# One block's lead for w_out's pieces, their split folded into the norm's scale, and the first transposes two steps later

## The chip, the cores and the metric

The kernel runs on one core of one Trainium2 chip. The metric is the device time of one execution in microseconds. TensorE multiplies matrices and transposes by a matmul with the identity, VectorE and ScalarE do the work on elements, GpSimd (POOL) takes a few small steps, and SyncE (SP) issues nearly all transfers from HBM. Each of these engines works through its own queue in the order in which the program was built.

## The reference

Attention of 2 x 12 heads over 448 tokens gives x of 896 x 768. Two feed-forward blocks follow; the change lies in the first:

```python
h = x @ w_in                                   # 896 x 1024
e = np.exp(h - h.max(-1, keepdims=True))
solu = h * e / (e.sum(-1, keepdims=True) + 1e-09)
ln = (solu - mean) / np.sqrt(var + 1e-06) * g_ln
x2 = ln @ w_out                                # 896 x 768
```

The second block is `(silu(x2 @ w_gate) * (x2 @ w_val)) @ w_out2`. The weights come as 64-bit floats.

## The kernel before

Every matmul operand is kept as two 32-bit words, a high one (rounded to the format that TensorE reads) and a low one (what the rounding left), and a product is made of three matmuls: high by high, high by low, low by high (`mm3`).

**Tiles.** The 896 tokens are seven blocks of 128, t = 0 to 6. `ff1_h(t)` makes h_t, two PSUM banks of 128 x 512, in six steps of six matmuls, one step for each 128 columns of x; the last step also issues the tail: maxima (VectorE), the negated maximum, two exponentials with their sums (ScalarE), the sum and its reciprocal, the product e_t = exp * 1/sum * h (VectorE, two halves), mean and variance, a power on GpSimd, and the norm of e_t in place. For t below 5 the variance comes from VectorE's statistics, for 5 and 6 from two squares on ScalarE; the norm itself is VectorE's for t below 4 and ScalarE's from 4 on.

`ff1_T(t)` transposes the normed e_t (eight 128 x 128 transposes into the two banks lt_t_0 and lt_t_1) and writes high (ScalarE) and low words (VectorE) into `lA` (blocks 0 to 2), `lB` (3 and 4) or `lC`, which is part of `y` (5 and 6).

`ff1_x2(j)` makes 128 columns of x2, j = 0 to 5, for the 384, 256 and 256 tokens of lA, lB and lC: 24 matmuls each, over eight pieces of w_out. `load_w_out(j)` prepares these: two transfers of 512 rows (i = 0, 1) into one of two `raw` buffers; `f32` turns the 64-bit words into 32-bit ones (ScalarE takes the magnitude; VectorE clamps, shifts and twice joins words) in one of two `f32` buffers; then, before the change, ScalarE scales each of the four 128 x 128 pieces in place by the norm's factors `gt`, ScalarE copies the 128 x 512 to the high words, VectorE subtracts to get the low ones. The tiles of w_out have three buffers, so w_out 3 lies where w_out 0 lay.

**Order.** Up to the end of attention the program keeps the order in which it is written. From line 541 on, `in_order` is off and the build's scheduler sorts each engine's instructions; the list `steps` (lines 563 and 568 to 574) sets their rank, so that a moved entry moves instructions on all engines. `pin=True` keeps the first steps of `f32` where they are written. The buffers `h`, `lt` and the x2 accumulators share eight PSUM banks.

In the second list the entries `wo[2]` to `wo[5]` stand one block ahead of their use:

```python
steps = x2[0][0] + x2[0][1] + wo[2] + x2[1][0] + T5 + x2[1][1] + T6 + x2[0][2] + x2[1][2]
for j in range(2, KD):
    if j + 1 < KD:
        steps += wo[j + 1]
```

In the names of rows a number counts tiles: `e_5_1760` is e of block 5, `wo_1_0` the second w_out's first half, `sm_t` the small sums of block t. In the profile's rows these numbers are left out.

Of the kernel before, what the change touches and what calls it, by code (L numbers as in the profile page):

```python
# [5 lines left out]
F32 = mybir.dt.float32  # L6
# [3 lines left out]
AF = mybir.ActivationFunctionType  # L10
ALU = mybir.AluOpType
# [25 lines left out]
class Kernel:  # L37
# [379 lines left out]
    def load_w_out(self, j):  # L417

        w = self.wos[j] = self.wo.tile([128, 2, self.K1, 128], F32R, name=f"wo_{j}", tag="wo")
        for i in range(2):  # L420
            c = slice(4 * i, 4 * i + 4)
            src = self.w_out[i * 512:(i + 1) * 512, j * 128:(j + 1) * 128].rearrange("(f p) d -> p f d", p=128)
            f = self.f32(self.load64(src, f"wo_{j}_{i}"), f"wo_{j}_{i}", pin=True).rearrange("p (f d) -> p f d", f=4)
            for m in range(4):
                self.A.activation(f[:, m], f[:, m], AF.Copy, scale=self.gt[:, 4 * i + m:4 * i + m + 1])
            self.hi_act(w[:, 0, c], f)
            self.lo_dve(w[:, 1, c], f, w[:, 0, c])

    def ff1_x2(self, j, get, N, o):

# [75 lines left out]
    def run(self):  # L506
        nc = self.nc
        KD, K1, K2, F1 = self.KD, self.K1, self.K2, self.F1
# [19 lines left out]
        w = [self.w_in_steps(i) for i in range(2 * KD)]  # L528
# [5 lines left out]
        h = [self.ff1_h(t) for t in range(7)]  # L534
# [16 lines left out]
        T = [self.ff1_T(t, lambda: lA, 128 * t) for t in range(3)]  # L551
# [5 lines left out]
        T3, T4 = self.ff1_T(3, lambda: lB, 0), self.ff1_T(4, lambda: lB, 128)  # L557
        T5, T6 = self.ff1_T(5, lambda: lC, 0), self.ff1_T(6, lambda: lC, 128)
        wo = [[(0.0, lambda j=j: self.load_w_out(j))] for j in range(KD)]
        blocks = ((lambda: lA, 384, 0), (lambda: lB, 256, 384), (lambda: lC, 256, 640))  # L560
        x2 = [[[self.ff1_x2(j, *blocks[n])] for n in range(3)] for j in range(KD)]

        steps = h[1] + T[0] + h[2] + T[1] + h[3][:2] + T[2] + h[3][2:] + h[4][:3] + wo[0] + h[4][3:] + wo[1] + h[5][:5] + T3 + h[5][5:] + h[6][:2] + T4 + h[6][2:]
        for _, f in steps:
            f()
        X = [self.slot(f"wi{u}", [128, 6144], f"x2_{u}") for u in range(2)]
        self.x2 = [X[j // 3][:, j % 3 * 1792:(j % 3 + 1) * 1792].rearrange("p (u n) -> p u n", u=2) for j in range(KD)]
        steps = x2[0][0] + x2[0][1] + wo[2] + x2[1][0] + T5 + x2[1][1] + T6 + x2[0][2] + x2[1][2]
        for j in range(2, KD):
            if j + 1 < KD:  # L570
                steps += wo[j + 1]
            if j >= KD - 2:
                steps += [(0.0, lambda i=j - KD + 2: self.load_gv(0, i))]
            steps += x2[j][0] + x2[j][1] + x2[j][2]
# [76 lines left out]
```

## Time and profile before

| | |
|---|---|
| median of 3 runs | 508.88 us (508.77 to 511.54) |
| the profiled execution: time | 509.66 us |
| its span, first to last instruction | 507.9 us |
| mean granted TensorE clock | 0.992 |
| TensorE busy | 98% of the span |
| VectorE busy | 69% |
| ScalarE busy | 51% |

Attention fills the span to about 121 us, h and x2 lie from there to about 242 us, the second feed-forward block behind. In the profile a wait is the idle time of an engine before an instruction, put down to the instruction that ended it. The chain that ended last names, for each moment, what the end of the kernel hung on. Nearly all matmuls are issued by one helper, so all of them have line 29; rows are told apart by tile names: `x` on `lA`, `lB` or `y` is a matmul of x2, `h` one of h, `lt` a transpose.

### The profile page before, as it was taken

To read this page: it belongs to the slowest core of one execution; us is meant where nothing else is said; L and a number is where in the kernel's file an instruction comes from. 1 tells how busy PE (TensorE), PEld (TensorE's weight loads), DVE (VectorE), ACT (ScalarE), POOL (GpSimd) and SP (SyncE) were. 2 spreads that over 40 slices of the span, in tenths; PEclk is the share of its full clock that TensorE was granted. 3 is DMA by queue.
4 is the path that set the end of the run, shared out by engine and by line. 5 is a ranking of instruction groups with operands and counts; after the bars stand their busy time and mean duration, and the time that the engine had idled before them with its cause. 6 is when DMAs were issued, how large, how long until landed. Compare 5 with 4: busy or idle time off the path is not lost.

```text
span 507.9 us, 7456 instructions
## 1 busy us (share of the span) xinstructions
PE 496.3 (98%) x2920; PEld 411.3 (81%) x2920; DVE 348.0 (69%) x625; ACT 256.7 (51%) x388; POOL 20.7 (4%) x63
## 2 busy tenths in 40 slices
PE   6999999999999999999999999999999999999996
PEld 5454444446788899999999988889999889999996
DVE  2788888873778895677899999897997868200000
ACT  2999999990313696474545454353444434100000
POOL 1111111110000000000000000000000000000000
PEclk8999999999999999999999999999999999999999
DMA  8955555320000222145354545435243525111111
GB/s 169 218 127 151 132 151 129 91 70 2 0 1 0 82 85 84 43 146 165 125 176 136 185 127 162 149 124 161 98 148 94 168 80 157 31 32 31 32 31 32
DMA packets 66916, 52.40 MB, mean 103 GB/s; under 512 B 35904, under 2 KB 62272, under 8 KB 66880
## 3 DMA queue, kind: packets, MB, share of 16 engines
q1 hardware_dynamic: 65184, 50.90, 35.5%
q10 hardware_dynamic: 1664, 1.02, 0.6%
q8 instruction: 23, 0.38, 0.3%
q14 instruction: 13, 0.11, 0.1%
q0 software_dynamic: 32, 0.00, 0.0%
HBM read 49.16 MB, written 2.75 MB: 102 GB/s over the span
## 4 chain that ended last, share of the span: by engine, by line
PE 93%; DMA 2%; ACT 2%; DVE 2%; issue 0%; ACTq 0%; POOL 0%; POOLq 0%
PE o L29 17%; PE g L29 17%; PE v L29 17%; PE x L29 10%; PE h L29 10%; PE pv L29 8%; PE sc L29 7%; PE S L29 4%; PE T L29 2%; DMA q<-in_q_dram 1%; PE lt L29 1%; DVE sm L29 1%; ACT P L29 1%; ACT wo L29 1%; DMA wo_raw<-in_moe_w_out_dram 1%; DVE e L29 0%
## 5 line engine op out<-in xcount | busy, mean ns | idle before, releaser
L29 PE MATMUL g<-x,y 128*128 128x512 f32 (+1 forms) x432 | 91.3, 363 | 0.0
L29 PE MATMUL v<-x,y 128*128 128x512 f32 (+1 forms) x432 | 90.5, 362 | 0.0
L29 PEld LDWEIGHTS g<-x,y 128*128 128x128 f32 x432 | 78.3, 188 | 8.8
L29 PEld LDWEIGHTS v<-x,y 128*128 128x128 f32 x432 | 78.2, 188 | 8.5
L29 PE MATMUL h<-wi,x 128*128 128x512 f32 x252 | 58.8, 392 | 0.0
L29 PEld LDWEIGHTS h<-wi,x 128*128 128x128 f32 x252 | 46.8, 188 | 10.9 <-issue 1.4
L29 PE MATMUL o<-x,a 128*128 128x384 f32 x294 | 52.4, 336 | 0.0
L29 PEld LDWEIGHTS o<-x,a 128*128 128x128 f32 x294 | 51.2, 188 | 0.0
L29 ACT ACTIVATE P<-sc,c 112x896 f32<-112x896 f32 x48 | 45.6, 999 | 3.1 <-PE sc L29 2.7
L29 ACT ACTIVATE P<-P,cp 112x1792 f32<-112x1792 f32 x24 | 43.1, 1795 | 0.5
L29 PE MATMUL pv<-P,v 112*64 112x448 f32 x192 | 41.2, 551 | 0.0
L29 PEld LDWEIGHTS sc<-ks 64*112 64x112 f32 x288 | 24.1, 176 | 19.6 <-issue 8.5
L493 ACT ACTIVATE ob<-o 128x384 f32<-128x384 f32 x14 | 6.9, 491 | 65.0 <-PE o L29 65.0
L29 PE MATMUL sc<-ks 64*112 64x448 f32 x288 | 36.8, 387 | 1.0 <-ACT P L29 1.0
L29 PE MATMUL o<-y,a 128*128 128x384 f32 x189 | 34.3, 337 | 0.0
L29 PEld LDWEIGHTS o<-y,a 128*128 128x128 f32 x189 | 33.2, 188 | 0.1
L29 PEld LDWEIGHTS pv<-P,v 112*64 112x64 f32 x192 | 11.7, 136 | 23.9 <-issue 16.6
L29 PE MATMUL x<-lA,wo 128*128 128x384 f32 x144 | 28.1, 337 | 0.9 <-ACT wo L29 0.9
L29 PEld LDWEIGHTS x<-lA,wo 128*128 128x128 f32 x144 | 24.3, 188 | 1.1 <-ACT wo L29 1.1
L29 ACT ACTIVATE a<-sg 128x384 fp32r<-128x384 f32 (+1 forms) x24 | 13.9, 578 | 21.9 <-DVE sg L469 21.8
L29 DVE SCALAR_TENSOR_TENSOR w<-w_raw,w 128x768 uint32<-128x768 uint32 (+1 forms) x26 | 23.1, 892 | 0.4
L29 ACT ACTIVATE wv<-wv_raw 128x768 f32<-128x768 f32 x12 | 10.9, 910 | 24.6 <-DMA wv_raw<-in_moe_w_val_dram 24.6
(97 smaller groups left out, 682.5 us busy)
## 6 DMA issues: line engine op xcount, KB each, us to landing
wg_raw<-in_moe_w_gate_dram SPq DMA_DIRECT2D x12, 768.0 KB, 4.3
wv_raw<-in_moe_w_val_dram SPq DMA_DIRECT2D x12, 768.0 KB, 4.3
w_raw<-in_moe_w_out_dram SPq DMA_DIRECT2D x11, 768.0 KB, 4.5
wi_raw<-in_moe_w_in_dram SPq DMA_DIRECT2D x12, 512.0 KB, 4.2
wo_raw<-in_moe_w_out_dram SPq DMA_DIRECT2D x12, 512.0 KB, 3.5
v<-in_v_dram SPq DMA_DIRECT2D x24, 112.0 KB, 2.8
k<-in_k_dram SPq DMA_DIRECT2D x23, 112.0 KB, 4.1
q<-in_q_dram SPq DMA_DIRECT2D x23, 112.0 KB, 4.6
```

The lines of the kernel that those rows point to most:

```text
L29: i = f(*a, **k)
L493: nc.scalar.activation(ob, acc, AF.Copy)
```

## The change

It has three parts. `load_w_out` no longer scales in place: ScalarE scales each 128 x 128 piece straight into the high words, and VectorE makes the low words of each piece in one instruction, (f * g) - high, so that the copy of 128 x 512 and the subtraction of 128 x 512 go and four instructions on 128 x 128 come. In the first list T[0] stands behind the first two steps of h[2] instead of behind h[1]. In the second list w_out 3 to 5 stand one block earlier: w_out 3 before the last block of x2_1, and w_out j + 2 before x2_j.

```diff
             for m in range(4):
-                self.A.activation(f[:, m], f[:, m], AF.Copy, scale=self.gt[:, 4 * i + m:4 * i + m + 1])
-            self.hi_act(w[:, 0, c], f)
-            self.lo_dve(w[:, 1, c], f, w[:, 0, c])
+                g, hi = self.gt[:, 4 * i + m:4 * i + m + 1], w[:, 0, 4 * i + m]
+                self.A.activation(hi, f[:, m], AF.Copy, scale=g)
+                self.V.scalar_tensor_tensor(w[:, 1, 4 * i + m], f[:, m], g, hi.bitcast(F32), op0=ALU.mult, op1=ALU.subtract)
...
-        steps = h[1] + T[0] + h[2] + T[1] + h[3][:2] + T[2] + h[3][2:] + h[4][:3] + wo[0] + h[4][3:] + wo[1] + h[5][:5] + T3 + h[5][5:] + h[6][:2] + T4 + h[6][2:]
+        steps = h[1] + h[2][:2] + T[0] + h[2][2:] + T[1] + h[3][:2] + T[2] + h[3][2:] + h[4][:3] + wo[0] + h[4][3:] + wo[1] + h[5][:5] + T3 + h[5][5:] + h[6][:2] + T4 + h[6][2:]
...
-        steps = x2[0][0] + x2[0][1] + wo[2] + x2[1][0] + T5 + x2[1][1] + T6 + x2[0][2] + x2[1][2]
+        steps = x2[0][0] + x2[0][1] + wo[2] + x2[1][0] + T5 + x2[1][1] + T6 + x2[0][2] + wo[3] + x2[1][2]
         for j in range(2, KD):
-            if j + 1 < KD:
-                steps += wo[j + 1]
+            if j + 2 < KD:
+                steps += wo[j + 2]
```

What this does to the engines' queues is seen at three places. The first is VectorE's queue around the norm of block 1 (`TENSOR_SCALAR e_1`, 128x1024); `lA<-lt_0` are the low halves of block 0's transposes, `TENSOR_REDUCE sm_2<-h_2` the maxima of block 2, and a minus marks the order before, a plus that of the change.

```order
+L29 TENSOR_TENSOR lA_1374<-lt_0_0_1453,lA_1374 128x4x128
+L29 TENSOR_TENSOR lA_1374<-lt_0_1_1460,lA_1374 128x4x128
 L29 BN_STATS sm_1_1421<-e_1_1422 128x6 x2
 L29 BN_AGGR sm_1_1421<-sm_1_1421 128x2
 L29 TENSOR_SCALAR sm_1_1421<-sm_1_1421 128x1 x2
+L29 TENSOR_REDUCE sm_2_1491<-h_2_0_1439 128x1
 L29 TENSOR_SCALAR e_1_1422<-e_1_1422,sm_1_1421 128x1024
-L29 TENSOR_REDUCE sm_2_1491<-h_2_0_1453 128x1
-L29 TENSOR_REDUCE sm_2_1491<-h_2_1_1454 128x1
+L29 TENSOR_REDUCE sm_2_1491<-h_2_1_1440 128x1
```

The two low halves now stand between block 1's product and its statistics (before, they stood ahead of the product), and the maximum of h_2's first half has moved ahead of e_1's norm.

The second place is ScalarE's queue around block 5's exponentials (`e_5<-h_5`), ahead of the transposes of block 4; `wo_1_0<-wo_1_0_raw` is the magnitude of w_out 1's first half. Before:

```order
L29 ACTIVATE lB_1381<-lt_3_1_1746 128x4x128
L29 ACTIVATE e_4_1661<-e_4_1661,sm_4_1660 128x1024
L29 ACTIVATE wo_1_0_1681<-wo_1_0_raw_1679 128x512
L29 ACTIVATE e_5_1760,sm_5_1759<-h_5_0_1707,sm_5_1759 128x512
L29 ACTIVATE e_5_1760,sm_5_1759<-h_5_1_1708,sm_5_1759 128x512
L29 ACTIVATE wo_0_1_1630<-wo_0_1_1630,gt_115 128x128 x4
L29 ACTIVATE wo_0_1613<-wo_0_1_1630 128x512
```

And now, the same place:

```order
L29 ACTIVATE lB_1381<-lt_3_1_1754 128x4x128
L29 ACTIVATE wo_0_1613<-wo_0_1_1632,gt_115 128x128 x4
L29 ACTIVATE e_5_1768,sm_5_1767<-h_5_0_1715,sm_5_1767 128x512
L29 ACTIVATE e_4_1665<-e_4_1665,sm_4_1664 128x1024
L29 ACTIVATE wo_1_0_1685<-wo_1_0_raw_1683 128x512
L29 ACTIVATE e_5_1768,sm_5_1767<-h_5_1_1716,sm_5_1767 128x512
```

The four scalings of w_out 0's second half moved from behind the two exponentials to ahead of them, and the norm of e_4 and a magnitude stand between the two.

The third place is VectorE's queue from block 5's small sums to its product (`e_5,sm_5<-e_5,sm_5,h_5`). Before:

```order
L29 TENSOR_SCALAR sm_5_1759<-sm_5_1759 128x1
L29 SCALAR_TENSOR_TENSOR wo_0_1_1630<-wo_0_1_raw_1628,wo_0_1_1630 128x512
L29 TENSOR_SCALAR wo_1_0_1681<-wo_1_0_1681 128x512 x2
L29 SCALAR_TENSOR_TENSOR wo_1_0_1681<-wo_1_0_raw_1679,wo_1_0_1681 128x512
L29 TENSOR_SCALAR sm_5_1759<-sm_5_1759 128x1
L29 SCALAR_TENSOR_TENSOR wo_1_0_1681<-wo_1_0_raw_1679,wo_1_0_1681 128x512
L29 RECIPROCAL sm_5_1759<-sm_5_1759 128x1
L29 SCALAR_TENSOR_TENSOR e_5_1760,sm_5_1759<-e_5_1760,sm_5_1759,h_5_0_1707 128x512
L29 SCALAR_TENSOR_TENSOR e_5_1760,sm_5_1759<-e_5_1760,sm_5_1759,h_5_1_1708 128x512
```

And now, from the clamp of w_out 1's first half (the first row) on:

```order
L29 TENSOR_SCALAR wo_1_0_1685<-wo_1_0_1685 128x512
L29 TENSOR_REDUCE sm_6_1837<-h_6_0_1785 128x1
L29 TENSOR_SCALAR wo_1_0_1685<-wo_1_0_1685 128x512
L29 TENSOR_SCALAR sm_5_1767<-sm_5_1767 128x1
L29 TENSOR_REDUCE sm_6_1837<-h_6_1_1786 128x1
L29 SCALAR_TENSOR_TENSOR wo_1_0_1685<-wo_1_0_raw_1683,wo_1_0_1685 128x512
L29 RECIPROCAL sm_5_1767<-sm_5_1767 128x1
L29 TENSOR_TENSOR lB_1381<-lt_4_0_1799,lB_1381 128x4x128
L29 TENSOR_TENSOR lB_1381<-lt_4_1_1806,lB_1381 128x4x128
L29 TENSOR_SCALAR sm_6_1837<-sm_6_1837 128x1
L29 SCALAR_TENSOR_TENSOR wo_1_0_1685<-wo_1_0_raw_1683,wo_1_0_1685 128x512
L29 SCALAR_TENSOR_TENSOR e_5_1768,sm_5_1767<-e_5_1768,sm_5_1767,h_5_0_1715 128x512
```

The product of e_5 stood ahead of the maxima of block 6; now both maxima, the words of w_out 1's first half and the low halves of lt_4 (`lB<-lt_4`) stand ahead of it.

In TensorE's queue lt_0 comes behind twelve matmuls of h_2, lt_1 right behind h_2 as before, and the same 60 matmuls of x2 stand between lt_4 and lt_5, in another order among themselves. SyncE's transfers of w_out stand as before.

## Rows read from the trace of the kernel before

**Rows 1.** Page section 1: engine, busy us (share of the span), instructions.

```profile
PE 496.3 (98%) x2920; PEld 411.3 (81%) x2920; DVE 348.0 (69%) x625; ACT 256.7 (51%) x388; POOL 20.7 (4%) x63
```

**Rows 2.** TensorE's waits in the whole span: total us, times, longest.

```profile
PE T L29 <- DMA q<-in_q_dram: 3.7, 1, 3.7
PE sc L29 <- ACT P L29: 1.0, 1, 1.0
PE warm L29 <- DVE z L29: 1.0, 1, 1.0
PE x L29 <- ACT wo L29: 0.9, 1, 0.9
PE lt L29 <- DVE e L29: 0.5, 1, 0.5
PE x L29 <- ACT y L29: 0.4, 1, 0.4
```

**Rows 3.** Timeline 134 to 143 us: start, us, engine, operation, [idle before].

```profile
134.50 1.28 DVE L29 TENSOR_REDUCE sm<-h 128x1 f32<-128x512 f32 x2
...
134.64 1.09 PE L29 MATMUL lt<-ident,e 128*128 128x128 f32 x8 [0.53 <-DVE e L29]
...
136.57 0.21 DVE L29 TENSOR_SCALAR sm<-sm 128x1 f32<-128x1 f32 x1
...
140.06 1.28 DVE L29 BATCH_NORM_STATS2 sm<-e 128x6 f32<-128x512 f32 x2
...
142.69 0.81 DVE L29 TENSOR_SCALAR e<-e,sm 128x1024 f32<-128x1024 f32 x1
```

**Rows 4.** Chain that ended last, in order of time: start, us, what.

```profile
135.73 8.20 PE h L29 x36
...
179.26 0.87 PE lt L29 x8
...
189.24 0.87 PE lt L29 x8
...
190.12 3.78 PE x L29 x26
```

**Rows 5.** Timeline 175 to 186 us, ScalarE and VectorE, same columns.

```profile
175.29 0.67 ACT L29 ACTIVATE e<-h,sm 128x512 f32<-128x512 f32 x1
...
176.62 1.28 ACT L29 ACTIVATE wo<-wo,gt 128x128 f32<-128x128 f32 x4
...
177.87 0.75 DVE L29 SCALAR_TENSOR_TENSOR e<-e,sm,h 128x512 f32<-128x512 f32 x1
...
184.89 1.26 ACT L29 ACTIVATE e<-e,sm 128x1024 f32<-128x1024 f32 x1
```

**Rows 6.** Operations by shape, ScalarE, 130 to 245 us: busy us, mean ns, idle before.

```profile
L29 ACT ACTIVATE wo<-wo_raw 128x512 f32<-128x512 f32 x12 | 7.9, 658 | 0.7 <-DMA wo_raw<-in_moe_w_out_dram 0.7
```

**Rows 7.** The same of VectorE, 130 to 245 us.

```profile
L29 DVE SCALAR_TENSOR_TENSOR wo<-wo_raw,wo 128x512 uint32<-128x512 uint32 x24 | 16.4, 687 | 0.3
...
L29 DVE TENSOR_TENSOR wo<-wo,wo 128x512 fp32r<-128x512 f32 x12 | 8.2, 687 | 6.7 <-ACT wo L29 6.7
...
L29 DVE TENSOR_REDUCE sm<-h 128x1 f32<-128x512 f32 x12 | 7.8, 684 | 0.9 <-PE h L29 0.9
...
L29 DVE TENSOR_SCALAR sm<-sm 128x1 f32<-128x1 f32 x28 | 5.4, 200 | 5.6 <-POOL sm L29 2.8 <-ACT e L29 2.6
...
L29 DVE TENSOR_SCALAR wo<-wo 128x512 f32<-128x512 f32 x12 | 5.1, 424 | 2.1 <-ACT wo L29 1.7
...
L29 DVE TENSOR_TENSOR x<-x,x 128x256 fp32r<-128x256 f32 x12 | 5.1, 422 | 4.2 <-ACT x L29 4.0
```

**Rows 8.** Page section 6, transfers: count, KB each, us to landing.

```profile
wo_raw<-in_moe_w_out_dram SPq DMA_DIRECT2D x12, 512.0 KB, 3.5
```

**Rows 9.** Stretches of us: busy us per engine, granted TensorE clock, DMA.

```profile
13.00:14.00 1.00, 1.00 (x7) 0.48 (x4) 0.95 (x2) 0.89 (x2) 0.00 (x0) 0.50 0.96 191
17.00:18.00 1.00, 0.58 (x6) 0.45 (x6) 0.97 (x3) 1.00 (x2) 0.00 (x0) 1.00 1.00 281
```

## Prediction

> **What bounds the kernel.** I read the page's busy shares first: TensorE works in 98% of the span [rows 1], so little can be saved beside it. Then TensorE's own waits: six, 7.5 us together [rows 2]. The 3.7 us for q, the 1.0 for the first scores and the 1.0 for the warm-up zeros lie ahead of all that changes. What the change can touch is 0.5 us before lt_0, 0.9 us where `x2_3` waits for w_out, and 0.4 us where `x2_0`'s last block waits for `y`: 1.8 us. To this comes that eight transposes after a wait take 1.09 us [rows 3] instead of 0.87 [rows 4]. The most to be gained is thus about 2 us, 0.4%. The loss has no such bound: everything from 121 to 242 us is one chain of matmuls, TensorE takes them in the order of the program, and a normed tile that comes late stops it. So I followed the two chains that end in a normed tile and that the change reorders, `e_1`'s and `e_5`'s, through VectorE and ScalarE.
>
> **Part 1: lt_0 behind 12 matmuls of h_2.** TensorE ends h_1 at 134.64 - 0.53 = 134.11 us [rows 2, 3]. Now 12 matmuls of h_2 follow, 2.7 us, and cover the rest of e_0's norm, which lt_0 awaited until 134.64. Gain: 0.53 + (1.09 - 0.87) = 0.75 us. If that cover were gone, this and no more would be lost.
>
> But lt_1 comes right behind h_2 and needs e_1 normed. TensorE is there at 134.11 + 8.20 (36 matmuls of h_2) + 0.87 (lt_0) = 143.18 [rows 4]. Before, e_1's norm began at 142.69 [rows 3]. Three changes in VectorE's order move it:
> - The low halves of lt_0 no longer stand between h_1's maxima (end 134.50 + 1.28 = 135.78) and the step after them (136.57 before): that step starts at 135.82, 0.75 earlier [rows 3].
> - They now stand between e_1's product and its statistics: two of 0.69 [rows 7], 1.28 together if they overlap as the two statistics do [rows 3], and 1.20 net of the joint behind them. That much later.
> - The maximum of h_2's first half now stands ahead of the norm. That half is ready at about 143.0, the norm's factors at 143.1; the maximum takes 0.68 [rows 7], part of it before the factors are there. 0.50 later.
>
> So the norm starts at 142.69 - 0.75 + 1.20 + 0.50 = 143.64, takes 0.81, ends at 144.45, and lt_1 starts at 144.51: a wait of 1.33, plus 0.22 for transposes from rest. Cost 1.55; with the gain of 0.75 TensorE is **0.80 us later** from here on. At lt_2, by the same steps, e_2 is normed at 153.1 and wanted at 144.51 + 1.09 + 8.20 = 153.8: no further wait.
>
> **Part 2: w_out split while it is scaled.** ScalarE loses a 128x512 copy per piece, twelve times. VectorE loses one 128x512 subtraction of 0.69 and gets four on 128 columns that no row shows. Below: 0.20, a step on one column; above: 0.42, 256 columns [rows 7]. From 256 to 512 columns the time grows by 0.265, so 128 take 0.29, and I use that since it lies on the line of the nearest rows. Four, each overlapping the next by 0.08, are 0.9 us: 0.2 more per piece (-0.1 to +0.75 at the bounds). "VectorE: DVE Perf Modes" of the Trainium skill gives, in its section on the TRN2 errata, a fixed 58 cycles per instruction, by which 128 columns are an estimated 0.19 us, and the wait found below would be some 0.4 shorter; it also warns that small tiles pay the fixed part each time.
>
> By itself that moves little. What matters is where the pieces stand in the queues. Times are now those of the changed kernel, 0.80 late.
> - Before, ScalarE did both exponentials of e_5 from 175.29 on and scaled w_out behind them, from 176.62 [rows 5]. Now the four scalings of w_out 0's second piece (1.28) stand ahead, and wait for VectorE's words until about 174.6. Then follow the first exponential, e_4's norm (1.26 like e_5's), the next piece's magnitude (0.66, [rows 6]) and the second exponential: e_5's sums are there at 179.1 instead of 176.7.
> - VectorE stands at the clamp of w_out 1 until that magnitude ends (178.3), and next at the maximum of h_6. Its first half ends 0.2 before h_6, so at 179.26 + 0.80 - 0.2 = 179.87 [rows 4]. From there to the end of e_5's product stand twelve instructions: two maxima (0.68), a shift (0.42), three steps of 0.20 at most, two word operations (0.69), the low halves of lt_4 (0.69), the two products (0.75) [rows 5, 7]. 6.6 us, less 0.08 at each of eleven joints: 5.7. The product ends at 185.6; before, it began at 177.87 [rows 5].
> - Then e_5's mean (186.1). ScalarE is in e_6's exponentials, four scalings, a magnitude and an eviction until 187.2; the two squares (like the exponentials, 0.67 each and a read) end at 188.7. VectorE's next small steps end at 189.3, GpSimd's power at 190.0, a word operation and the factors at 191.0; ScalarE's norm takes 1.26 [rows 5]. e_5 is normed at 192.3, and **lt_5 starts at 192.35**.
>
> TensorE wants lt_5 at 189.24 + 0.80 = 190.04 [rows 4], behind the same 60 matmuls. The wait is 2.3 us, with the slower transposes **2.5 us**. With the bounds of the four small subtractions on this chain, 2.2 to 3.1; if VectorE gains 1 us elsewhere, 1.5.
>
> **Part 3: pieces one block sooner.** Behind lt_5 the engines have caught up: e_6 is normed 3.6 us before lt_6, and the 0.37 us for `y` shrink to 0.2, so -0.2. The third buffer of w_out is that of w_out 0, so piece 3's low halves wait for the end of x2_0's last block (205.6). But x2_3 now starts at 214.8, and its second piece, scaled at about 215.6, is wanted 12 matmuls of 384 and 10 of 256 columns later, some 3.2 us (26 such take 3.78, [rows 4]), at 218.0. The wait of 0.88 goes: -0.9, with 2.4 us to spare. SP issues the transfers in the same order, each when one of two raw buffers is free; the tightest is w_out 2's first, which lands 3.5 us [rows 8] after 184.3, at 187.8, and is wanted at 188.9. The gate and value weights lie under x2_4 and x2_5, some 20 us, as before; without that cover each would cost a transfer's time. Behind 242 us TensorE waits for nothing [rows 2], so that stage only starts later.
>
> **Sum.** -0.75 + 1.55 + 2.5 - 0.2 - 0.9 = +2.2 to +2.3 us: span 507.9 to 510.2. The profiled execution took 509.66 us, the median of the three runs is 508.88; from the median, **511.2 us**.
>
> **The rivals.**
> - *All is gained* (faster): e_5's chain isn't blocked, and -0.75 - 0.37 - 0.88 = -2.0 gives 506.9 us. It decides if e_5's product ends before 183.3 and e_1's norm before 143.2. For it: VectorE idles at 143.7 before, so there is some room. Against it: the order puts VectorE's waits for a magnitude and for h_6 ahead of e_5's sum.
> - *Only the first new wait stays*: lt_5 waits 0 to 0.3, so +0.80 + 0.1 - 0.2 - 0.9 = -0.2, 508.7 us. For it: my walk has some 40 joints, and 0.06 less at each would do. Against it: at two places VectorE stands still, and there no joint is gained.
> - *TensorE's clock falls before lt_5.* At the start TensorE rested 3.7 us [rows 2], and until 14.6 us it then ran at a granted clock of 0.50, the 1.2 GHz level [rows 9]. After the rest of 1.0 before 17.4 it stayed at 1.00 [rows 9]. A rest of 2.3 lies between. From 9.06 to 14.6 half of 5.5 us was lost, so +2.7: 513.9 us. "TensorE: Matmul & The Clock Gate" of the Trainium skill, section "What's actually happening", calls the half rate the default that activity lifts; no row here shows a rest between 1.0 and 3.7.
>
> **How the numbers follow.** The forecast (a loss of 1 to 3.5 us, 509.9 to 512.4) gets 0.60; only the first wait 0.16; all gained 0.08; the clock 0.16. The range from 508.4 to 513.9 leaves out the 506.9 and half of the clock's case, about 0.16. 1%, about what a measurement of this kernel can tell from no change, is 5.1 us. No case reaches 503.8, and half of the clock's lies beyond 513.9: faster 0.01, same 0.91, slower 0.08.
>
> **What would show it.** TensorE's waits should list two for `lt`: about 1.3 near 144.5, and about 2.3 near 192.3 on ScalarE's `e`; none of `x` on `wo`. lt_0 should start at about 136.8 with no wait, and VectorE stand idle near 177 and 179. I am wrong if lt_5 starts before 191, if TensorE still waits for w_out, or if the granted clock falls behind 192.

## The result and the profile after

The changed kernel takes 512.14 us (median of 20 runs, 510.55 to 515.73) and the kernel before 508.91 beside it (20 runs, 508.59 to 512.65). The ratio is 1.0054, with a 95% interval from 1.0039 to 1.0070: a loss of 2.75 us (2.0 to 3.6), which counts as the same time here. A ratio in this text is taken over all runs of both kernels; it is not the quotient of the two medians, which is 1.0063 here (3.2 us). The forecast was 511.2 us, a loss of 2.2 to 2.3.

The profiled execution spans 510.6 us, 2.7 more than before. Page section 1 of the kernel after, which answers to [rows 1] (busy us, share of the span, instructions): TensorE's work is the same, VectorE has 4.8 us more, ScalarE 6.5 us less.

```profile
PE 496.1 (97%) x2920; PEld 411.0 (80%) x2920; DVE 352.8 (69%) x661; ACT 250.2 (49%) x376; POOL 21.9 (4%) x63
```

TensorE's waits of the kernel after, which answer to [rows 2] (total us, times, longest):

```profile
PE T L29 <- DMA q<-in_q_dram: 4.4, 2, 3.8
PE lt L29 <- ACT e L29: 2.3, 1, 2.3
PE lt L29 <- DVE e L29: 1.3, 1, 1.3
...
PE x L29 <- ACT y L29: 0.2, 1, 0.2
```

Against [rows 2], lt_0's 0.5 and `x2_3`'s 0.9 on w_out are gone, and two waits of normed tiles are new: 1.3 and 2.3 us. The two rows left out, for the first scores and the warm-up, and the wait for q lie in the start, which differs from one execution to the next. To leave it out I measure between two places of TensorE's chain: the first 18 matmuls of h_0 and the first of g. These are the rows of the chain and of the timeline, first before, then after (start us, us, what):

```profile
112.54 4.30 PE h L29 x18
242.20 3.29 PE L29 MATMUL g<-x,y 128*128 128x384 f32 x18
```

```profile
113.13 4.30 PE h L29 x18
244.98 3.29 PE L29 MATMUL g<-x,y 128*128 128x384 f32 x18
```

From the one to the other it is 129.66 us before and 131.85 after: **+2.19**. The changed execution reached h_0 0.59 us later already, so 0.59 is to be taken off its times before they are set against the prediction's. Behind g both take the same (507.9 - 242.2 = 265.7, 510.6 - 245.0 = 265.6).

The first new wait, on VectorE and TensorE (timeline: start, us, engine, operation, [idle before]):

```profile
139.90 1.28 DVE L29 TENSOR_TENSOR lA<-lt,lA 128x512 fp32r<-128x512 f32 x2
141.10 1.28 DVE L29 BATCH_NORM_STATS2 sm<-e 128x6 f32<-128x512 f32 x2
...
143.61 0.68 DVE L29 TENSOR_REDUCE sm<-h 128x1 f32<-128x512 f32 x1
144.21 0.81 DVE L29 TENSOR_SCALAR e<-e,sm 128x1024 f32<-128x1024 f32 x1
...
145.07 1.09 PE L29 MATMUL lt<-ident,e 128*128 128x128 f32 x8 [1.32 <-DVE e L29]
```

lt_0's low halves (139.90) stand ahead of e_1's statistics and h_2's maximum (143.61) ahead of its norm, and lt_1 starts behind that norm. The second, on ScalarE, VectorE and TensorE, same columns:

```profile
175.19 1.28 ACT L29 ACTIVATE wo<-wo,gt 128x128 fp32r<-128x128 f32 x4 [3.40 <-DVE wo L29]
176.37 0.67 ACT L29 ACTIVATE e<-h,sm 128x512 f32<-128x512 f32 x1
...
178.72 0.67 ACT L29 ACTIVATE e<-h,sm 128x512 f32<-128x512 f32 x1
```

```profile
175.72 1.13 DVE L29 SCALAR_TENSOR_TENSOR wo<-wo,gt,wo 128x128 fp32r<-128x128 f32 x4
178.85 0.43 DVE L29 TENSOR_SCALAR wo<-wo 128x512 f32<-128x512 f32 x1 [1.99 <-ACT wo L29]
180.45 0.69 DVE L29 TENSOR_REDUCE sm<-h 128x1 f32<-128x512 f32 x1 [1.17 <-PE h L29]
...
184.69 0.74 DVE L29 SCALAR_TENSOR_TENSOR e<-e,sm,h 128x512 f32<-128x512 f32 x1
```

```profile
191.67 1.24 ACT L29 ACTIVATE e<-e,sm 128x1024 f32<-128x1024 f32 x1 [0.20 <-DVE sm L29]
...
192.96 1.09 PE L29 MATMUL lt<-ident,e 128*128 128x128 f32 x8 [2.33 <-ACT e L29]
```

Against [rows 5], the four scalings of w_out 0 have moved ahead of e_5's exponentials; VectorE stands still 1.99 us for a magnitude (178.85) and 1.17 for h_6's maximum (180.45), and begins e_5's product at 184.69 instead of 177.87.

### The profile page after: what moved, and what is told of

Its sections match the earlier page's. It is cut to its first block, busy times and chain, and to the rows that moved or that the text cites. A ratio compares the mean times of both kernels' runs of the same rounds, so it can differ in the third digit from the quotient of the medians.

```text
span 510.6 us, 7490 instructions
## 1 busy us (share of the span) xinstructions
PE 496.1 (97%) x2920; PEld 411.0 (80%) x2920; DVE 352.8 (69%) x661; ACT 250.2 (49%) x376; POOL 21.9 (4%) x63
## 3 DMA queue, kind: packets, MB, share of 16 engines
HBM read 49.16 MB, written 2.75 MB: 102 GB/s over the span
## 4 chain that ended last, share of the span: by engine, by line
PE 90%; DVE 5%; DMA 2%; ACT 1%; issue 0%; POOL 0%; ACTq 0%; SPq 0%; POOLq 0%
PE o L29 17%; PE g L29 17%; PE v L29 17%; PE x L29 10%; PE h L29 8%; PE pv L29 8%; PE sc L29 6%; PE S L29 4%; DMA q<-in_q_dram 2%; PE T L29 2%; DVE sm L29 2%; DVE e L29 1%; PE lt L29 1%; DVE wo L29 1%; ACT e L29 1%
## 5 line engine op out<-in xcount | busy, mean ns | idle before, releaser
L29 ACT ACTIVATE e<-h,sm 128x512 f32<-128x512 f32 x14 | 9.5, 683 | 30.0 <-DVE sm L29 30.0
```

What stands on the lines that cost most here:

```text
L29: i = f(*a, **k)
```

## The experiments

In the table, "h_0 to g" is the distance above less the 129.66 us of before; the columns behind it are TensorE's waits in us (e5 to e7 also wait 0.4 at lt_2). *clock* marks a profile in which the granted clock fell to 0.50 behind such a wait.

| kernel | ratio to before (95%) | h_0 to g | lt_0 | lt_1 | lt_5 | lt_6 | x2_0 on y | x2_3 on w_out |
|---|---|---|---|---|---|---|---|---|
| before | | 0 | 0.53 | 0 | 0 | 0 | 0.37 | 0.88 |
| the change | 1.0054 (1.0039 to 1.0070) | +2.19 | 0 | 1.32 | 2.33 | 0 | 0.25 | 0 |
| e1 part 1 | 1.0003 (0.9985 to 1.0021) | +0.65 | 0 | 1.32 | 0 | 0 | 0.38 | 0.74 |
| e2 part 2 | 1.0068 (1.0047 to 1.0089) | +3.56 | 0.53 | 0 | 2.32 | 0 | 2.32 | 0 |
| e3 part 3 | 0.9966 (0.9948 to 0.9983) | -1.17 | 0.53 | 0 | 0 | 0 | 0.37 | 0 |
| e4 part 2, w_out 1 later | 1.0078 (1.0050 to 1.0105) | +4.23, clock | 0.53 | 0 | 4.10 on w_out ahead of it | 0 | 0 | 0 |
| e5 part 1, order held | 1.0040 (1.0023 to 1.0058) | +3.45, clock | 0 | 0 | 0 | 1.69 | 0.73 | 0.53 |
| e6 = e5 and e3 | 1.0034 (1.0020 to 1.0047) | +2.59, clock | 0 | 0 | 0 | 1.69 | 0.73 | 0 |
| e7 = e6, w_out 2 to 5 split | 1.0020 (1.0007 to 1.0033) | +0.55 | 0 | 0 | 0 | 1.69 | 0.25 | 0 |
| e8 change, w_out 0 and 1 unsplit | 0.9996 (0.9986 to 1.0006) | -0.30 | 0 | 1.31 | 0 | 0 | 0.25 | 0 |
| e9 lt_0 beside lt_1 | 0.9990 (0.9981 to 0.9998) | -0.63 | 0 | 0 | 0 | 0 | 0.37 | 0.91 |
| e10 = e9 and e3 | 0.9955 (0.9942 to 0.9968) | -1.85 | 0 | 0 | 0 | 0 | 0.37 | 0 |
| e11 parts 1 and 2 | 1.0055 (1.0040 to 1.0070) | +3.89, clock | 0 | 1.32 | 2.32 | 0 | 0.25 | 0 |
| e12 the change again | 1.0067 (1.0044 to 1.0090) | +3.72, clock | 0 | 1.31 | 2.32 | 0 | 0.25 | 0 |

**The parts alone.** e1, e2 and e3 each apply one part of the diff to the kernel before: the new `steps` line of the h stage, the new loop in `load_w_out`, and the two lines that give w_out 3 to 5.

> The first edit alone: the first normed tile's transposes behind twelve matmuls of h_2, w_out prepared and issued as before. My theory (order on VectorE): lt_0 waits 0 instead of 0.53 us, lt_1 waits 1.3 us because lt_0's two low halves and h_2's first maximum stand ahead of e_1's norm; with the slower restart of the transposes (0.22 us, gone at lt_0 and new at lt_1) the time is 0.8 us above before (+0.16%, ratio 1.0010 to 1.0025). lt_5 (no wait), x2_3 (0.88 us on w_out) and x_0_640 (0.37 us on y) stay as they are. Rival (the edit does what it says): lt_1 waits 0 and the time is 0.75 us below before (ratio 0.9985). Rival (something beyond the waits makes the whole change dearer than its 2.2 us, its 20 runs lay 3.2 us above before): this part alone already costs over 1.5 us.

The median is 509.55 us against 508.79. The time alone does not decide, since its interval holds no change too; the waits do, and so does the distance of +0.65:

```profile
135.39 1.03 PE L29 MATMUL lt<-ident,e 128*128 128x128 f32 x8
143.20 1.09 PE L29 MATMUL lt<-ident,e 128*128 128x128 f32 x8 [1.32 <-DVE e L29]
```

lt_0 no longer waits, and lt_1 waits 1.32 with w_out prepared as before. So the first new wait belongs to part 1 alone.

> The second edit alone: w_out split into its two halves while the norm's scale is applied, in columns of 128, with the first normed tile and w_out's pieces given where they were. My theory (order): ScalarE takes the four scalings of w_out 0's second piece ahead of e_5's exponentials, VectorE takes the words of w_out 1, both maxima of h_6 and lt_4's low halves ahead of e_5's product, and lt_5 waits 2.3 us on e_5 (2.0 to 2.7), as it did in the whole change; lt_0 keeps its 0.53 us. x2_3's wait of 0.88 us on w_out, which the pieces given sooner removed in the whole change, stays within 0.9 us. Time 2.3 to 2.7 us above before (ratio 1.0045 to 1.0055). Rival (VectorE's added work: 0.45 us in each of twelve pieces is what costs): waits for w_out spread over the x2 stage, at x2_2 and later, 1 us or more in all, and lt_5 waits under 1 us. Rival (no effect): all hidden, within 0.3 us of before.

512.73 us against 508.79. The wait of lt_5 came as expected, but the time lies above what was expected, and two waits were missed: `x2_0`'s last block waits 2.32 us for `y`, and `x2_3` no longer waits for w_out. ScalarE and TensorE in e2:

```profile
200.82 1.28 ACT L29 ACTIVATE wo<-wo,gt 128x128 fp32r<-128x128 f32 x4 [0.96 <-DVE wo L29]
202.00 1.05 ACT L29 ACTIVATE y<-lt 128x512 fp32r<-128x512 f32 x2
...
202.62 0.50 PE L29 MATMUL x<-y,wo 128*128 128x256 f32 x2 [2.32 <-ACT y L29]
```

The same place on ScalarE in the whole change:

```profile
199.48 0.60 ACT L29 ACTIVATE y<-lt 128x512 fp32r<-128x512 f32 x1
200.71 1.28 ACT L29 ACTIVATE wo<-wo,gt 128x128 fp32r<-128x128 f32 x4 [0.63 <-DVE wo L29]
```

In e2 four scalings of w_out 2, which wait for VectorE, stand ahead of both halves of `y`; in the change the first half stands ahead of them. Part 1, which edits only the h stage 60 us earlier, is what sets that order otherwise: e11, parts 1 and 2 without part 3, waits 0.25 there like the change. So the price of part 2 depends on part 1: the parts' distances add to 0.65 + 3.56 - 1.17 = 3.04 and the change has 2.19.

> The third edit alone: w_out 3, 4 and 5 given one block sooner, all else as before. My theory: only x2_3's wait of 0.88 us on w_out goes, every other wait as before (lt_0 0.53, x_0_640 on y 0.2 to 0.4): 0.9 us below before (ratio 0.9975 to 0.9990). Rival (the pieces given sooner get in the way): the steps of w_out 3 stand ahead of e_6's norm or of y's halves on ScalarE and VectorE, lt_6 or x_0_640 waits 0.5 to 2 us more, and the time is the same or up to 1.5 us above before. Rival (the transfer is what is late, not the place): x2_3 still waits 0.5 us or more.

507.49 us against 508.79. The gain is a little more than expected (ratio 0.9966 against 0.9975 to 0.9990). Only that wait is gone, and it is worth 1.17 us, 0.3 more than it lasted. TensorE's rows show most of the 0.3. First before, then e3, the same two matmuls of `x2_3`:

```profile
217.60 0.61 PE L29 MATMUL x<-lA,wo 128*128 128x384 f32 x2 [0.88 <-ACT wo L29]
```

```profile
214.43 1.54 PE L29 MATMUL x<-y,wo 128*128 128x256 f32 x12
215.81 0.51 PE L29 MATMUL x<-lA,wo 128*128 128x384 f32 x2
```

Without a wait the two start 0.16 us before the matmuls ahead of them end (214.43 + 1.54 - 215.81), and they take 0.10 less. A wait loses both: 0.88 + 0.16 + 0.10 = 1.14.

**Order or work.** e4 is e2 with `wo[1]` moved:

```
-        steps = h[1] + T[0] + h[2] + T[1] + h[3][:2] + T[2] + h[3][2:] + h[4][:3] + wo[0] + h[4][3:] + wo[1] + h[5][:5] + T3 + h[5][5:] + h[6][:2] + T4 + h[6][2:]
+        steps = h[1] + T[0] + h[2] + T[1] + h[3][:2] + T[2] + h[3][2:] + h[4][:3] + wo[0] + h[4][3:] + h[5][:5] + T3 + h[5][5:] + wo[1] + h[6][:2] + T4 + h[6][2:]
```

> The second edit alone as in e2 (the split while scaling, all twelve pieces, the same VectorE work), but w_out 1 is given behind h_5 instead of ahead of it. In the new order only four scalings and one subtraction of w_out 0's second piece are left near e_5's exponentials, and of w_out 1 nothing stands ahead of e_5's product or norm; the first maximum of h_6 still does. My theory (what costs in e2 is where w_out 1's steps stand in the two engines' order): lt_5 waits under 0.8 us, 0.5 of it for that maximum, and the time falls by 1.5 us or more against e2, unless w_out 1, now later, is waited for at x2_1 (its first matmuls stand right behind lt_5; if so, a wait of 1 to 4 us shows there on w_out, and the verdict goes by lt_5's own wait). Rival (VectorE's added work of 0.45 us in each piece is what costs): lt_5 still waits 1.5 us or more, the time is as in e2.

513.23 us. e_5's norm, and then TensorE:

```profile
185.15 1.24 ACT L29 ACTIVATE e<-e,sm 128x1024 f32<-128x1024 f32 x1
...
190.25 0.65 PE L29 MATMUL x<-lA,wo 128*128 128x384 f32 x2 [4.10 <-ACT wo L29]
190.71 1.91 PE L29 MATMUL lt<-ident,e 128*128 128x128 f32 x8
```

With all the work of the split, e_5 is normed at 186.39, 8.3 us behind lt_4's start (178.08); in e2 lt_5 starts 12.5 us behind lt_4's (193.41 and 180.93). TensorE came at 190.25 - 4.10 = 186.15, so lt_5 alone would have waited some 0.3 us. So the added work of the split, spread over all pieces, does not by itself make e_5 late; what stands ahead of e_5's steps does. The edit also takes w_out 1's words out of e_5's way, which stood there before as well, so it does not set order against work by itself; the trace of the change does that below. It gains nothing here: w_out 1 is now late itself, `x2_1` stands 4.10 us on it ahead of lt_5, and the clock falls.

e8 undoes the split for w_out 0 and 1 only, in the whole change:

```
+            if j < 2:
+                for m in range(4):
+                    self.A.activation(f[:, m], f[:, m], AF.Copy, scale=self.gt[:, 4 * i + m:4 * i + m + 1])
+                self.hi_act(w[:, 0, c], f)
+                self.lo_dve(w[:, 1, c], f, w[:, 0, c])
+                continue
             for m in range(4):
...
```

> The whole change with one thing undone: w_out 0 and 1 are prepared as before (scaling in place, copy, subtraction of 512 columns), w_out 2 to 5 are split while scaling. The first normed tile and the pieces are as in the change, VectorE's order is free. My theory: e_5's exponentials are ahead of w_out 0's scalings again and its product ahead of h_6's maxima, though the two loads' words still stand ahead of that product; lt_5 waits 0 to 0.6 instead of 2.33, lt_1 keeps its 1.3; time 2.0 to 2.6 us below the change, so -0.3 to +0.5 against before (ratio 0.9990 to 1.0010). Rival (lt_5's wait comes from the first normed tile's new place or the pieces given sooner, not from the split): lt_5 still waits 1.5 us or more and the time is that of the change (ratio 1.005).

508.81 us against 509.10, as expected. One wait of normed tiles is left, lt_1's of 1.31 us.

Eight of the twelve pieces are still split and cost nothing that shows. The whole of lt_5's wait came from the split of w_out 0 and 1, whose steps stand among e_5's. e8 takes back their work and their order together.

**Can part 1's wait be mended?** e5 is e1 with VectorE held in written order over the first 24 steps:

```
-            if self.kernel.in_order:
+            if self.kernel.in_order or (self.kernel.pin_v and self.engine is self.kernel.nc.vector):
...
-        for _, f in steps:
+        for n, (_, f) in enumerate(steps):
+            self.pin_v = n < 24
             f()
+        self.pin_v = False
```

> The first edit alone as in e1, but VectorE keeps the order in which the code is written from h_1 to lt_2's low halves and h_3 (TensorE's and ScalarE's rows stay free): e_1's norm stands ahead of lt_0's two low halves and of h_2's maxima, and e_2's norm ahead of h_3's maxima. The work is the same, and lt_0 stands at the same place behind twelve matmuls. My theory (what costs in e1 is the order on VectorE): lt_0 and lt_1 both wait 0, lt_2 waits 0 to 0.5; time 0.75 us below before (ratio 0.9975 to 0.9995), 1.4 us below e1. Rival (the place itself costs, because the transposes' results take slots or VectorE time that e_1 or e_2 need): lt_1 or lt_2 still waits 1 us or more and the time is not below before.

511.90 us against 509.10: the expectation was wrong. lt_1 does not wait, as I said; but lt_2 waits 0.41, and the loss comes 50 us later. TensorE, then ScalarE, at lt_6:

```profile
196.45 1.09 PE L29 MATMUL lt<-ident,e 128*128 128x128 f32 x8 [1.69 <-ACT e L29]
198.27 0.79 PE L29 MATMUL x<-y,wo 128*128 128x256 f32 x2 [0.73 <-ACT y L29]
```

```profile
193.60 0.49 ACT L29 ACTIVATE x<-x 128x384 fp32r<-128x384 f32 x1 [1.20 <-PE x L29]
193.99 1.27 ACT L29 ACTIVATE wo<-wo,gt 128x128 f32<-128x128 f32 x4
194.15 0.21 DVE L29 TENSOR_SCALAR sm<-sm 128x1 f32<-128x1 f32 x1 [0.44 <-POOL sm L29]
195.16 1.23 ACT L29 ACTIVATE e<-e,sm 128x1024 f32<-128x1024 f32 x1
```

And ScalarE before, with VectorE's step that ends the norm's factors:

```profile
191.19 1.28 ACT L29 ACTIVATE wo<-wo,gt 128x128 f32<-128x128 f32 x4
191.68 0.20 DVE L29 TENSOR_SCALAR sm<-sm 128x1 f32<-128x1 f32 x1
192.38 1.23 ACT L29 ACTIVATE e<-e,sm 128x1024 f32<-128x1024 f32 x1
193.92 0.49 ACT L29 ACTIVATE x<-x 128x384 fp32r<-128x384 f32 x1 [0.30 <-PE x L29]
```

Before, e_6's norm began at 192.38 and ended 1.3 us ahead of lt_6. Four scalings of w_out 2 stand right ahead of it in both kernels. Two things differ: the norm's factors are done at 194.36 instead of 191.88, and a copy of x2's 384 columns, for which ScalarE stands 1.20 us, has moved from behind the norm to ahead of the scalings. TensorE wanted lt_6 at 196.45 - 1.69 = 194.76. With ScalarE free at 194.36 the norm would have ended at some 195.6, so by an estimate 0.9 us of the wait come from the late factors and 0.8 from the scalings behind that copy. Nothing is held at that place: the scheduler chose another order there when only the h stage was changed. And the clock fell behind the two waits.

> A version that could beat both: w_out 3 to 5 given one block sooner as in e3, the first normed tile behind twelve matmuls of h_2 with VectorE held in written order as in e5, and w_out prepared as before (no split while scaling). My theory: the waits of lt_0 (0.53 and 0.22 of slower transposes) and of x2_3 (0.88) both go, x_0_640 keeps 0.2 to 0.4 on y; time 1.6 to 2.0 us below before (ratio 0.9960 to 0.9970), 0.7 below e3. Rival (the freed time turns up as a new wait): lt_6 or x_0_640 waits 0.7 us or more, and the time is that of e3 or above.

510.80 us: the rival named for it came true, with the same two waits as in e5.

> The kernel of e6 with the split while scaling for w_out 2 to 5 only; w_out 0 and 1, whose steps stand among e_5's in the order of ScalarE and VectorE, are prepared as before. So eight of twelve pieces carry VectorE's added 0.45 us and save ScalarE's copy of 0.63. My theory (the split costs by its place among e_5's steps, not by its work): lt_5 waits 0, no wait on w_out in the x2 stage, the time is that of e6 within 0.3 us. Rival (VectorE's added work costs): waits for w_out at x2_2 to x2_5 or a later x_0_640, 0.5 us or more above e6. Rival (ScalarE's saved copies gain): x_0_640's wait on y of 0.37 goes and the time is 0.4 us below e6.

510.26 us. lt_6 waits 1.69 as in e6, which I had not foreseen; `x2_0`'s wait for `y` is 0.25 instead of 0.73 and the clock does not fall. The time is 0.5 us below e6 and not within 0.3, near to what the second rival named (0.4 less, with the wait for `y` gone); how much of it is the clock and how much the saved copies was not taken apart. No wait for w_out shows, so the eight split pieces cost nothing here either.

e9 looks for another place for lt_0, one that leaves the order behind lt_3 alone:

```
-        steps = h[1] + T[0] + h[2] + T[1] + h[3][:2] + T[2] + h[3][2:] + h[4][:3] + wo[0] + h[4][3:] + wo[1] + h[5][:5] + T3 + h[5][5:] + h[6][:2] + T4 + h[6][2:]
+        steps = h[1] + h[2] + T[0] + T[1] + h[3][:2] + T[2] + h[3][2:] + h[4][:3] + wo[0] + h[4][3:] + wo[1] + h[5][:5] + T3 + h[5][5:] + h[6][:2] + T4 + h[6][2:]
```

> The first edit alone, but with lt_0's transposes behind all six steps of h_2, right ahead of lt_1's, instead of behind two (order on VectorE free, w_out as before). In the new order nothing of lt_0 stands ahead of e_1's norm; its two low halves stand behind h_2's maxima, beside lt_1's, where e_2's exponentials are waited for; from lt_3 on both engines' rows stay as before but for a few of w_out 0's. My theory (in e1 lt_0's low halves and h_2's maximum in e_1's chain were the cause; in e5 it was the new order behind lt_3): lt_0 and lt_1 wait 0, e_2's exponentials come 1.1 to 1.5 us later behind lt_0's high halves, which lt_2's spare of 0.9 us and the 0.9 us of lt_0's transposes now ahead of it cover: lt_2 waits 0 to 0.4. lt_5 and lt_6 wait 0. Time 0.4 to 0.75 us below before (ratio 0.9985 to 0.9992). Rival (the low halves in any later place cost the next chain what they cost here): lt_2 waits 0.8 us or more, the time is that of before or above.

508.65 us against 509.25, as expected. e10 adds part 3.

> e9 with e3: lt_0's transposes right ahead of lt_1's, and w_out 3 to 5 given one block sooner; w_out prepared as before. My theory: the waits of lt_0 (0.53, and 0.22 of slower transposes) and of x2_3 (0.88 and the restart behind it, together 1.0 to 1.2) both go, no new one comes: 1.5 to 2.0 us below before (ratio 0.9960 to 0.9972), the fastest of the study. Rival (as in e6 a change ahead of lt_3 sets the scheduler's order behind it anew): a wait of 0.7 us or more at lt_5, lt_6 or x_0_640, and the time is not below e3 (ratio 0.9966 there).

506.89 us against 509.25, 2.3 us (1.6 to 2.95) faster than before: the fastest kernel of the study. TensorE at lt_0 with lt_1, and at lt_2:

```profile
143.00 1.91 PE L29 MATMUL lt<-ident,e 128*128 128x128 f32 x16
153.02 1.06 PE L29 MATMUL lt<-ident,e 128*128 128x128 f32 x8
```

None waits. Of the 1.78 us of waits that the change was after, 1.41 are gone, and none is new.

**What part 3 gave.** In e2 `x2_3`'s wait had gone without part 3, so e11 takes part 3 out of the change, with the change itself (e12) on the same chip.

> The change without its third edit: lt_0 behind twelve matmuls of h_2 and the split while scaling, but w_out 3 to 5 given where they were. In e2 x2_3's wait on w_out was gone without that edit, because TensorE came there 4 us later. New theory: in the change TensorE comes 3.1 us late to x2_3 by lt_1 and lt_5, that alone covers the 0.88 us that w_out was late, and the third edit gives nothing there: x2_3 waits under 0.2 us, lt_1 1.3, lt_5 2.3, x_0_640 0.25, as in the change, and the time is that of the change within 0.3 us. Rival (my prediction's step: the third edit takes the 0.9 us away): x2_3 waits 0.7 us or more and the time is 0.9 to 1.2 us above the change.

> The whole change on the same chip, to stand beside e11. From its first profile TensorE loses 2.2 us between the first matmuls of h_0 and the first of g; its runs gave 2.75 us above before (interval 2.0 to 3.6). If the waits are all there is, the ratio is 1.0040 to 1.0050 and the profile again has 2.1 to 2.3 us more than before between those two points, with the start differing by up to 3 us either way. If there is a cost besides, the ratio is 1.0055 or more and these two points lie over 2.6 us further apart than before.

511.42 us (e11) and 512.13 (e12) against 508.77. TensorE's waits of e11 behind the start are the same three as in the list of the change: `lt` 2.3 and 1.3, `x` on `y` 0.2. No wait for w_out: the third edit is worth 1.17 us alone and at most 0.2 in the change (from `x2_0`'s last block to g it is 45.01 us in e11, 44.84 in e12), where TensorE comes to `x2_3` 3 us late by itself. And e12 answers its own question with "a cost besides": h_0 to g is +3.72, 1.53 more than in the first profile, with the same waits to 0.01 us. lt_5 in e12, and its stretches of time (us, busy per engine, granted clock, DMA):

```profile
191.18 1.65 PE L29 MATMUL lt<-ident,e 128*128 128x128 f32 x8 [2.32 <-ACT e L29]
```

```profile
191.00:192.00 1.00, 0.82 (x6) 0.82 (x7) 0.56 (x2) 1.00 (x5) 0.86 (x1) 0.78 0.01 3
...
193.00:194.00 1.00, 1.00 (x7) 1.00 (x6) 0.80 (x4) 1.00 (x3) 0.00 (x0) 0.50 0.87 305
...
195.00:196.00 1.00, 1.00 (x8) 1.00 (x8) 1.00 (x4) 1.00 (x3) 0.00 (x0) 1.00 1.01 357
```

The same place of the change's first profile:

```profile
193.00:194.00 1.00, 1.00 (x9) 1.00 (x10) 0.56 (x3) 1.00 (x5) 0.64 (x1) 1.00 0.16 36
```

Behind the same rest of 2.3 us the granted clock fell to 0.50 (the 1.2 GHz level) for some 3 us in e12 and e11, and stayed at 1.00 in the first profile and in e2.

## Why the prediction was right, and where not

- **Part 1** (net +0.80, lt_1 at 144.51 with a wait of 1.33): measured 145.07 - 0.59 = 144.48 and 1.32. e1, e5 and e9 show the reason: with lt_0's low halves and h_2's maximum out of e_1's chain, by VectorE's order alone (e5) or by lt_0's place (e9), the wait is gone. e1's distance is +0.65, and 0.14 of the difference is `x2_3`'s shorter wait.
- **The 0.22 for a restart** is right as a sum and wrongly named. The 1.09 is of the timeline, the 0.87 of the chain, whose rows begin only where the one ahead ends. In the timeline eight transposes take 1.03 us without a wait and 1.09 behind one (both rows of e1); the other 0.16 is the overlap with the matmul ahead, which a wait loses, as at `x2_3` in e3.
- **Part 2** (lt_5 at 192.35, a wait of 2.3, with the slower transposes 2.5): measured 192.96 - 0.59 = 192.37, 2.33. e8 shows that the split of w_out 0 and 1 is the whole cause, e4 that e_5 is in time once w_out 1's steps stand elsewhere, and the next point that the small subtractions themselves are little of it.
- **The small subtraction** was estimated at 0.29 us, and four at 0.9. The row of the kernel after (operations by shape on VectorE, 130 to 245 us: busy us, mean ns, idle before):

```profile
L29 DVE SCALAR_TENSOR_TENSOR wo<-wo,gt,wo 128x128 fp32r<-128x128 f32 x48 | 14.4, 347 | 0.3
```

  0.347 us, and four in a row 1.13. It lies within the bounds of 0.20 to 0.42, and the estimate was 0.06 too low each. The estimated 0.19 us that "VectorE: DVE Perf Modes" of the Trainium skill would give is too low by almost half.

  I had put four of them on e_5's chain, and four stand there, between e_5's mean and the step with its variance (VectorE of the kernel after, and the last step of ScalarE's squares):

```profile
186.15 0.34 DVE L29 SCALAR_TENSOR_TENSOR wo<-wo,gt,wo 128x128 fp32r<-128x128 f32 x1
...
186.60 0.60 DVE L29 SCALAR_TENSOR_TENSOR wo<-wo,gt,wo 128x128 fp32r<-128x128 f32 x2
...
188.45 0.35 DVE L29 SCALAR_TENSOR_TENSOR wo<-wo,gt,wo 128x128 fp32r<-128x128 f32 x1
...
189.04 0.19 ACT L29 ACTIVATION_READ_ACCUMULATOR h<-e,sm 128x1 f32 x1
...
189.52 0.33 DVE L29 TENSOR_SCALAR sm<-sm 128x1 f32<-128x1 f32 x2
```

  But the variance also needs ScalarE's squares, which ended at 189.23; with 0.59 taken off that is 188.64, and 188.7 was forecast. So these four can have delayed it by 0.3 us at most, and the small ones ahead of 180.45 by nothing, since VectorE stands still there until TensorE's h_6 comes. The rest of the 2.33 is order. That the small ones took longer did not show in lt_5 because the squares came when forecast.
- **Part 3** (-0.9 at `x2_3`, -0.2 at `y`): the waits did go, 0.88 and 0.12, but the step that put the 0.9 down to the third edit failed. e11 has the same without it. I moved `x2_3` 3 us later in the sum, found w_out there in time, and did not ask whether it would have been in time in its old place. That the sum still came out is luck at this step: the wait goes either way.
- **Sum** +2.2 to 2.3: the first profile gives -0.53 - 0.22 (lt_0) + 1.32 + 0.22 (lt_1) + 2.33 + 0.22 (lt_5) - 0.12 (`y`) - 1.03 (from `x2_0`'s last block to g, 45.88 before and 44.85 after) = +2.19.
- **The clock rival** got 0.16 and 513.9 us. It is a matter of the execution: the same kernel shows it in e12, where the sign of being wrong "if the granted clock falls behind 192" came true, and not in its first profile. Where it came it cost 1.5 us, not 2.7 (e12: 3.72 - 2.19; e11: 3.89 - 2.19, less the 0.17 behind `x2_0` that it lacks of part 3). How often it comes is not settled, but each run has a mean granted clock over its span, and a fall to 0.50 for 3 us takes 0.003 off it. In 3 of the 20 runs of the change this mean is 0.998 or more, so such a fall did not come; they took 511.4 to 511.8 us, and those 21 of the 84 runs of the kernel before, beside e1 to e12, that have such a clock took 508.7 to 510.0, on average 2.4 less. In 7 of the 20 it is 0.989 or less, and these took 512.2 to 515.7; of the 84 there is 1. The start lowers the same mean, so a single run cannot be told by it; but it fits that the fall puts the median, 512.1, above the sum's 511.2.
- The two rivals in which less is lost are refuted by lt_1's and lt_5's waits in every profile of the change.

## What to carry to other kernels

Where a scheduler sets the order, an edit's price is not its instructions but the rows it moves, also 50 us further on: e5 mended the wait it aimed at and came out 3.45 us late by waits elsewhere and a fall of the clock, e9 moved the same tile to a place that left the rest alone and kept its gain. Before an edit is credited with a wait that goes, ask whether the wait would go anyway because the bounding engine now comes late. And a tile that is normed late is paid twice: the wait, and with some chance a stretch at half the clock behind it.

## What the runs showed of the hardware

- A rest of 2.3 us may or may not cost the clock: the granted clock fell to 0.50 in two of four profiles with that rest at lt_5. It also fell behind 4.10 us (e4) and in e5, behind 1.69 and then 0.73 us:

```profile
199.00:200.00 1.00, 1.00 (x5) 1.00 (x4) 1.00 (x3) 0.00 (x0) 0.00 (x0) 0.50 0.08 16
```

  It did not fall behind 1.69 and 0.25 us (e7), nor behind two rests of 2.32 us nine us apart (e2).
- A `scalar_tensor_tensor` of 128x128 on VectorE takes 0.347 us, and of 128x512 words 0.687 [rows 7]: four small ones cost 1.13 us where one subtraction of 512 columns cost 0.69.
- Taking a wait of 0.88 us off TensorE's chain brought 1.0 to 1.2 us (e3, e10 and the change). A wait costs its length, 0.16 us of overlap between matmuls, and 0.06 to 0.10 for slower first ones (lt_1 in e1, `x2_3` before and in e3).
